# Another order of the first loads and other planner numbers in a fused attention and gMLP kernel

## Chip, core and metric

The kernel runs on one core of a Trainium2 chip. The metric is the device time of one execution in microseconds; lower is better. A program of this kind has one launch, and all inputs start in the chip's main memory.

## The reference

Chunked attention (batch 4, 8 heads, 768 positions, head size 64) feeds a gMLP block. Each chunk of 32 queries sees 16 positions to its left, itself, 8 to its right, and 8 memory keys of its head.

```python
for c in range(nc):                       # 24 chunks
    k_full = concat([mem_k, k[l_start:r_end]]); v_full = concat([mem_v, v[l_start:r_end]])
    a = softmax(scale * q_c @ k_full.T)
    out[c] = a @ v_full
x = out, heads side by side               # [4, 768, 512]
h = relu(x @ w_in)                        # w_in [512, 1024]
u, v = h[..., :512], h[..., 512:]
v_n = (v - mean(v)) / sqrt(var(v) + 1e-6)
v_s = einsum('ts,bsd->btd', w_spatial, v_n) + b_spatial
return (u * v_s) @ w_out                  # w_out [512, 512]
```

w_in and w_out come in 64-bit floats; the kernel makes them 32-bit.

## The kernel before

**Tiles.** The tokens go through attention in 24 tiles of four chunks (128 positions, all heads): per tile a burst of 64 small matmuls for the scores of tile i and 64 for the values of tile i-1 (`burst`, line 419), a softmax on VectorE and ScalarE (lines 472 to 493), two transposes (lines 507 and 523), and the result x split into a rounded high and a low half (lines 528 and 532), since each product is made of three matmuls: high by high, low by high, high by low. Queries and keys come in groups of two tiles (`load_qk`), and group 0 in two units of one tile. Values come per tile (`load_v`, four or more DMAs).

**gMLP.** `ffn_v` multiplies a tile of x by the v half of w_in (four chunks of 128 rows by three matmuls, lines 561 to 563, 512 columns each), and its result is normalized and stored to main memory (`vn_far`). `ffn_u` multiplies three tiles of x by a quarter of the u half (384 columns), with chunks 0 to 3 in this order too. Later phases read both back (`near_v`, `near_u`) for the spatial product and the output product, each in seven partial products instead of eight (line 710).

**w_in.** `w_in_part(c, part, ...)` loads one part, rows c of four and the half `part` (0 is u, 1 is v), 512 KB as 64-bit words, into one of four `big` buffers, and makes 32-bit values: a scale on ScalarE (line 864), two shift operations on VectorE (lines 873, 874), a second scale on ScalarE (869), an addition on GpSimd (879), which frees the `big` buffer; then a rounded high half on ScalarE (893) and a low half (897), on VectorE for v-parts and on GpSimd for u-parts. The arguments after c and part are the rank of this work, the rank of the load and the engine of the low half.

**The order.** Nothing runs in the order of the source. `Plan.op` collects every operation with an engine, an expected time, what it reads and writes, and a rank. `Plan.order` then simulates the engines: each time it takes the operation that can start first, and among equals the lowest rank. What comes out is the order in which each engine's instructions are issued; on the chip each engine keeps to it and waits on semaphores. So an expected time that is off doesn't change what is computed, only what stands ahead of what. A load's expected end is the end of a pipe that moves `mb * drag / rate` us for each transfer, plus `landing`. Loads with `seq=True` keep the order of the source on SP's queue; each loop or call that makes them stands at the end of the file (lines 968 to 1003). `alone` keeps a VectorE operation from starting in the plan while GpSimd is busy, and GpSimd from starting until it ends; the two first shift operations are one planned operation of this kind.

**Pacing.** `held_by` limits what is in flight: a transfer waits until so many of the earlier ones have landed that it and the rest are within a window of megabytes. The window goes by what has been issued so far. The same function makes real waits in `transfer` and expected ones in the plan. q and k count 1.15 times their size, v 1.2 times.

**Filler.** Where the plan leaves TensorE idle between 9 and 36 us, `busy` (line 252) issues matmuls on the identity.

Of the kernel before, what the change touches and what calls it, by code (L numbers as in the profile page):

```python
# [10 lines left out]
U32 = mybir.dt.uint32  # L11
# [8 lines left out]
SLOT = 40  # L20
LEFT = 16
WIN = 64
MIDDLE = (38.0, 1.2)
PIECES = 4
NEG = -1.0e30

# [1 line left out]
class Plan:  # L28
# [111 lines left out]
    def held_by(self, flight, mb, none):  # L140

        moved = sum(size for _, size in flight)
        window = self.early[1] if moved <= self.early[0] else MIDDLE[1] if moved < MIDDLE[0] else self.window
        for back, (name, size) in enumerate(reversed(flight), 1):
            mb += size
            if back == 8 and moved > self.early[0] or mb > window:
                return name
        return none
# [10 lines left out]
def tile_chunked_attention_gmlp(  # L159
# [43 lines left out]

    sizes = {"f": 3, "sx": 1, "pt": 1, "xt": 1, "y": 5, "st": 9, "big": 4, "uo": 2, "x": 2, "vm": 3,
             "q": 2, "k": 2, "kT": 2, "p": 1, "xs": 1, "pT": 1, "vr": 2, "op": 4, "sm": 2, "ug": 6, "ot": 11}
    plan = Plan(sizes, {"f", "y", "st", "big", "ot"}, rate=0.30, landing=2.5, lat=0.06, window=1.75, early=(9.0, 2.0))
    op = plan.op

    def act(n):
# [56 lines left out]
    def src(t, offset, ap):  # L266
        return bass.AP(tensor=t.tensor, offset=offset, ap=ap)
# [20 lines left out]
    def load(dst, src_, w, rank, r=(), eng="SP", slow=1.0, us=0.45, seq=False, drag=1.0, of=None):  # L288
        e = {"SP": nc.sync, "ACT": nc.scalar, "POOL": nc.gpsimd}[eng]
        n = 4  # L290
        for s in src_.shape:
            n *= s
        mb = n / 1e6 * slow
        n = op(eng, us, lambda: transfer(e, dst() if callable(dst) else dst, src_, mb, of), r=r, w=w, rank=rank, mb=mb,
               after=line.get(eng) if seq else None, drag=drag)
        if seq:
            line[eng] = n
# [15 lines left out]
    def load_qk(g, units=(0, 1), seq=True):  # L313
        i = 2 * g
        b, c0 = i // UB, (i % UB) * UC
        off = b * H * D * S + c0 * CH
        nk = 2 * UT + CH
        lo = LEFT if c0 == 0 else 0
        hi = nk - LEFT if c0 + 2 * UC == NC else nk
        q0, q1 = units[0] * UT, units[-1] * UT + UT  # L320
        k0, k1 = max(lo, q0 + (CH if q0 else 0)), min(hi, q1 + CH)
        u = units[0]
        ks = ("k", g)
        n = PIECES if g > 1 else 1
        for t in range(n):
            ts = slice(t * T // n, (t + 1) * T // n)
            load(lambda ts=ts: spot("q", g, [P, T, 2 * UT])[:, ts, q0:q1],
                 src(q, off + q0 + ts.start * P * S, [[S, P], [P * S, T // n], [1, q1 - q0]]), w=[("q", g, u, t)], rank=10.0 * i,
                 slow=1.15, seq=seq)
        for t in range(n):  # L330
            ts = slice(t * T // n, (t + 1) * T // n)
            load(lambda ts=ts: spot("k", g, [P, T, nk])[:, ts, k0:k1],
                 src(k, off - LEFT + k0 + ts.start * P * S, [[S, P], [P * S, T // n], [1, k1 - k0]]), w=[("k", g, u, t)],
                 rank=10.0 * i, slow=1.15, seq=seq)

        def pad():
            a = t_["k", g]
            if k0 == lo > 0:
                nc.gpsimd.memset(a[:, :, 0:lo], 0.0)
            if k1 == hi < nk:  # L340
                nc.gpsimd.memset(a[:, :, hi:nk], 0.0)
        if k0 == lo > 0 or k1 == hi < nk:
            op("POOL", 0.2, pad, w=[ks + (u, "pad")], rank=10.0 * i, after=len(plan.ops) - 1)
# [203 lines left out]
    seq = [0]  # L547
# [305 lines left out]
    def from_f64(name, src_, rank, load_rank, home, after=()):  # L853
        big = ("big", *name)
        zk = ("st", ("z", name))

        def get():
            a = alloc("big", big, [P, 2 * DH], U32).rearrange("p (c w) -> p c w", w=2)
            t_[big] = a
            return a  # L860
        load(get, src_.bitcast(U32).rearrange("p (c w) -> p c w", w=2), w=[("big", big)], r=after, rank=load_rank, seq=True)

        def scale_():
            nc.scalar.activation(alloc("st", ("z", name), [P, DH], F32), t_[big][:, :, 1].bitcast(F32), AF.Copy,
                                 scale=2.0 ** -112)

        def rest():
            a = t_[big][:, :, 0]
            nc.scalar.activation(a, a, AF.Copy, scale=2.0 ** -29)

        def shift():
            zu = t_["st", ("z", name)].bitcast(U32)
            nc.vector.tensor_scalar(zu, zu, 3, None, op0=ALU.logical_shift_left)  # L873
            nc.vector.scalar_tensor_tensor(zu, t_[big][:, :, 1], 0x80000000, zu,  # L874
                                           op0=ALU.bitwise_and, op1=ALU.bitwise_or)

        def add():
            zu = t_["st", ("z", name)].bitcast(U32)
            nc.gpsimd.tensor_tensor(t_[big][:, :, 1] if home else zu, zu, t_[big][:, :, 0], op=ALU.add)
        op("ACT", 0.66, scale_, r=[("big", big)], w=[zk], rank=rank)  # L880
        op("DVE", 1.12, shift, r=[("big", big)], w=[zk], rank=rank, alone=True)
        op("ACT", 0.66, rest, r=[("big", big)], w=[("big", big, "r")], rank=rank)
        op("POOL", 1.6 if home else 1.35, add, r=[("big", big, "r"), zk] if home else [("big", big, "r")],
           w=[("big", big)] if home else [zk], rank=rank)
        if home:
            return (lambda: t_[big][:, :, 1].bitcast(F32)), ("big", big)
        return (lambda: t_["st", ("z", name)]), zk
# [14 lines left out]
    def w_in_part(c, part, rank, load_rank, sub_eng):  # L902
        cols = slice(part * DH, (part + 1) * DH)
        z, zk = from_f64(("win", c, part), w_in[c * P:(c + 1) * P, cols], rank, load_rank, False)
        split(sub_eng, DH, lambda x: (win_l if x else win_h)[:, c, cols], z, [zk], [("win", c, part)], rank)
# [64 lines left out]
    for j in range(NV):  # L970
        spread_mem(j, "DVE" if j < 1 else "POOL", 1.0 + 10 * j)
    load_qk(0, (0,))
    load_qk(0, (1,))
    w_in_part(0, 1, 5.0 + 0, 2.0 + 0, "DVE")
    w_in_part(1, 1, 5.0 + 1, 2.0 + 1, "DVE")
    w_in_part(2, 1, 5.0 + 2, 2.0 + 2, "DVE")
    w_in_part(3, 1, 5.0 + 3, 2.0 + 3, "DVE")
    load_v(0)
    load_qk(1)
    w_in_part(0, 0, 25.0 + 0, 15.0 + 0, "POOL")  # L980
    load_v(1)
    w_in_part(1, 0, 25.0 + 1, 15.0 + 1, "POOL")
    load_v(2)
    w_in_part(2, 0, 25.0 + 2, 15.0 + 2, "POOL")
    w_in_part(3, 0, 25.0 + 3, 15.0 + 3, "POOL")
    for j in range(NK):
        spread_keys(j, 1.0 + j)
    for i in range(NU + 1):
# [23 lines left out]
    for b in range(B + 1):  # L1012
        if b < B:
            rank = 300.0 + 10 * b
# [67 lines left out]
```

## Time and profile before

| what | us |
|---|---|
| median of 3 runs | 379.18 |
| lowest and highest of these | 376.54, 381.41 |
| the profiled execution | 375.05 |
| its span, first to last instruction | 373.3 |
| mean granted clock of TensorE in it | 0.999 of full speed |

The span is the part of the profiled execution that its rows describe. PE is the matrix engine (TensorE), PEld its loading of weights, DVE is VectorE, ACT ScalarE, POOL GpSimd, SP the engine that issues most DMAs; a q behind an engine's name is its queue. In a row `win_l<-st,win_h` names the written tile first.

### The profile page before, as it was taken

The page shows a single profiled execution, that of the slowest core. Times are in us where ns is not written, and L with a number is a line of the kernel's source. Part 1 is how long each engine was busy: PE and PEld are TensorE (multiplying, and loading weights), DVE is VectorE, ACT ScalarE, POOL GpSimd, SP SyncE. Part 2 cuts the span into 40 slices and gives each one's busy share as a digit, 9 for nine tenths or more (in the row PEclk, how much of TensorE's full clock was granted, in tenths as well). Part 3 has the DMA queues.
Part 4 walks back from the last instruction along what each step waited for, and adds up shares of the span by engine and source line. Part 5 has one row for each costly group of instructions (what it writes and reads, how often), then busy time and mean ns, then how long its engine had stood idle before and what let it go on. Part 6 is the DMA issues. An engine that isn't in the chain of part 4 may idle for free.

```text
span 373.3 us, 11922 instructions
## 1 busy us (share of the span) xinstructions
PE 355.9 (95%) x4988; PEld 326.7 (88%) x4988; DVE 285.0 (76%) x479; ACT 187.1 (50%) x334; POOL 160.5 (43%) x155
## 2 busy tenths in 40 slices
PE   2987989999999999999999999999999999999995
PEld 2865877998988978979889898999999999999995
DVE  3888856748758568566598589999969896898893
ACT  3768435454555454554473355346434743744371
POOL 6446642374386077520042194961256025106500
PEclk9999999999999999999999999999999999999999
DMA  8995888778787765886742648205720662230014
GB/s 230 316 260 140 232 257 210 235 217 220 228 251 214 249 212 147 274 232 194 216 163 93 246 137 311 88 2 173 246 90 3 207 217 84 84 130 2 0 54 159
DMA packets 48517, 65.52 MB, mean 176 GB/s; under 512 B 5456, under 2 KB 39888, under 8 KB 48464
## 3 DMA queue, kind: packets, MB, share of 16 engines
q1 hardware_dynamic: 47808, 64.44, 56.5%
q8 instruction: 39, 0.64, 0.8%
q10 hardware_dynamic: 656, 0.33, 0.3%
q14 instruction: 14, 0.11, 0.1%
HBM read 45.88 MB, written 18.87 MB: 173 GB/s over the span
## 4 chain that ended last, share of the span: by engine, by line
PE 83%; DVE 11%; ACT 2%; issue 2%; DMA 1%; SPq 0%; ACTq 0%; DVEq 0%
PE y L710 21%; PE f L710 15%; PE f L561 12%; PE f L562 11%; PE f L563 11%; PE sx L419 9%; PE xt L523 3%; PE pt L507 3%; DVE op L690 2%; DVE sm L673 2%; DMA k<-in_k_dram 1%; DVE st L874 1%; DVE st L873 1%; DVE wout L897 1%; DVE p L480 1%
## 5 line engine op out<-in xcount | busy, mean ns | idle before, releaser
L710 PE MATMUL y<-wsp,op 128*128 128x384 f32 x288 | 52.0, 336 | 0.9 <-ACT st L750 0.9
L764 POOL TENSOR_TENSOR ug<-st,ug 128x384 f32<-128x384 f32 x24 | 36.0, 1513 | 38.4 <-DVE st L756 34.4
L710 PEld LDWEIGHTS y<-wsp,op 128*128 128x128 f32 x288 | 49.9, 188 | 1.2 <-ACT st L750 1.2
L561 PE MATMUL f<-x,win_h 128*128 128x384 f32 x128 | 46.1, 360 | 0.0
L563 PE MATMUL f<-x,win_h 128*128 128x384 f32 x128 | 43.2, 337 | 0.0
L562 PE MATMUL f<-x,win_l 128*128 128x384 f32 x128 | 43.1, 337 | 0.0
L561 PE MATMUL f<-win_h,x 128*128 128x512 f32 x96 | 40.8, 425 | 0.0
L710 PE MATMUL f<-wsp,op 128*128 128x384 f32 x216 | 39.4, 336 | 0.0
L562 PE MATMUL f<-win_h,x 128*128 128x512 f32 x96 | 37.9, 394 | 1.0 <-DVE x L532 1.0
L563 PE MATMUL f<-win_l,x 128*128 128x512 f32 x96 | 37.7, 392 | 0.0
L710 PEld LDWEIGHTS f<-wsp,op 128*128 128x128 f32 x216 | 37.6, 188 | 0.0
L690 DVE TENSOR_TENSOR op<-sm,op 128x768 fp32r<-128x768 f32 x32 | 34.7, 1093 | 3.1 <-ACT op L687 2.6
L710 PE MATMUL y<-wout,op 128*128 128x256 f32 x288 | 35.9, 281 | 0.5 <-DVE op L690 0.5
L459 DVE TENSOR_TENSOR xs<-sx,rec 128x512 f32<-128x512 f32 x24 | 16.5, 687 | 25.1 <-PE sx L419 25.0
L710 PEld LDWEIGHTS y<-wout,op 128*128 128x128 f32 x288 | 34.7, 188 | 1.0 <-DVE op L690 0.8
L770 POOL TENSOR_TENSOR st<-st,bias 128x384 f32<-128x384 f32 x14 | 18.6, 1337 | 37.2 <-ACT st L750 28.4
L597 POOL TENSOR_TENSOR rstd<-ve,mhalf 128x1 f32<-128x1 f32 x24 | 14.7, 611 | 44.7 <-DVE ve L593 43.6
L687 ACT CAST op<-sm 128x768 fp32r<-128x768 f32 x32 | 26.2, 837 | 11.6 <-DVE sm L673 10.2
L419 PEld LDWEIGHTS sx<-kmain,q 64*32 64x32 f32 x1536 | 17.0, 107 | 14.8 <-issue 11.7
L622 ACT ACTIVATE uo<-f 128x384 f32<-128x384 f32 x32 | 15.6, 492 | 25.2 <-PE f L563 21.9
L398 POOL COPY vmain<-memv 8x1024 f32<-8x1024 f32 x22 | 23.9, 1090 | 10.0 <-PE sx L419 7.8
L419 PE MATMUL sx<-kmain,q 64*32 64x64 f32 x1536 | 20.9, 228 | 7.3 <-ACT kmain L404 7.0
(86 smaller groups left out, 770.6 us busy)
## 6 DMA issues: line engine op xcount, KB each, us to landing
vmain<-in_v_dram SPq DMA_DIRECT2D x48, 128.0 KB
vn_far<-st SPq DMA_DIRECT2D x24, 256.0 KB
u_far<-uo SPq DMA_DIRECT2D x32, 192.0 KB
vr<-vn_far SPq DMA_DIRECT2D x8, 768.0 KB
ug<-u_far SPq DMA_DIRECT2D x16, 384.0 KB
q<-in_q_dram SPq DMA_DIRECT2D x40, 128.0 KB
vmain<-in_v_dram SPq DMA_DIRECT2D x47, 96.0 KB
out_dram<-ot SPq DMA_DIRECT2D x33, 128.0 KB
```

The source lines that it names most:

```text
L398: ins = {"DVE": nc.vector, "POOL": nc.gpsimd}[eng].tensor_copy(to, of)
L419: ins = nc.tensor.matmul(o, w_, m, start=True, stop=True, skip_group_check=True)
L459: nc.vector.tensor_tensor(xs.rearrange("p t r d -> p r t d"), t_["sx", i][:, :, 1], rec.rearrange("p t r -> p r t").unsqueeze(3).broadcast ...
L561: nc.tensor.matmul(o, lh, rh, start=(j == 0), stop=False)
L562: nc.tensor.matmul(o, ll, rh, start=False, stop=False)
L563: nc.tensor.matmul(o, lh, rl, start=False, stop=(j == len(pairs) - 1))
L622: op("ACT", act(HT), lambda: nc.scalar.activation(alloc("uo", i, [P, HT], F32), t_["f", n], AF.Relu), r=[("f", n)], w=[("uo", i)], rank=rank)
L687: nc.scalar.copy(half(0), of())
L690: nc.vector.tensor_tensor(half(1), of(), half(0).bitcast(F32), op=ALU.subtract)
L710: nc.tensor.matmul(o, x, y, start=first and m == 1, stop=m == 3 * chunks, skip_group_check=True)
L764: nc.gpsimd.tensor_tensor(g, t_[st(x)], g, op=ALU.mult)
L770: {"DVE": nc.vector, "POOL": nc.gpsimd}[eng].tensor_tensor(a, a, bias[:, 1], op=ALU.add)
```

## The change

The first loads get another order: u-part 2 of w_in comes second among w_in's parts, both v-part 0 and u-part 2 ahead of unit 1 of the first queries and keys; v-part 1 comes behind the first values; u-part 0 becomes the last. The ranks of u-parts go from 25 + c to 28 + c. In the planner a landing takes 2.0 us instead of 2.5, the 64-bit loads of w_in and w_out are expected to take 0.7 of the time by size, and the narrow window of 1.2 MB begins at 10.5 MB moved instead of 9.0 (between them the window is 1.75 MB).

```diff
--- before.py
+++ after.py
@@ -20,7 +20,7 @@
 SLOT = 40
 LEFT = 16
 WIN = 64
-MIDDLE = (38.0, 1.2)
+MIDDLE = (10.5, 38.0, 1.2)
 PIECES = 4
 NEG = -1.0e30
 
@@ -140,7 +140,7 @@
     def held_by(self, flight, mb, none):
 
         moved = sum(size for _, size in flight)
-        window = self.early[1] if moved <= self.early[0] else MIDDLE[1] if moved < MIDDLE[0] else self.window
+        window = self.early[1] if moved <= self.early[0] else MIDDLE[2] if MIDDLE[0] < moved < MIDDLE[1] else self.window
         for back, (name, size) in enumerate(reversed(flight), 1):
             mb += size
             if back == 8 and moved > self.early[0] or mb > window:
@@ -203,7 +203,7 @@
 
     sizes = {"f": 3, "sx": 1, "pt": 1, "xt": 1, "y": 5, "st": 9, "big": 4, "uo": 2, "x": 2, "vm": 3,
              "q": 2, "k": 2, "kT": 2, "p": 1, "xs": 1, "pT": 1, "vr": 2, "op": 4, "sm": 2, "ug": 6, "ot": 11}
-    plan = Plan(sizes, {"f", "y", "st", "big", "ot"}, rate=0.30, landing=2.5, lat=0.06, window=1.75, early=(9.0, 2.0))
+    plan = Plan(sizes, {"f", "y", "st", "big", "ot"}, rate=0.30, landing=2.0, lat=0.06, window=1.75, early=(9.0, 2.0))
     op = plan.op
 
     def act(n):
@@ -858,7 +858,7 @@
             a = alloc("big", big, [P, 2 * DH], U32).rearrange("p (c w) -> p c w", w=2)
             t_[big] = a
             return a
-        load(get, src_.bitcast(U32).rearrange("p (c w) -> p c w", w=2), w=[("big", big)], r=after, rank=load_rank, seq=True)
+        load(get, src_.bitcast(U32).rearrange("p (c w) -> p c w", w=2), w=[("big", big)], r=after, rank=load_rank, seq=True, drag=0.7)
 
         def scale_():
             nc.scalar.activation(alloc("st", ("z", name), [P, DH], F32), t_[big][:, :, 1].bitcast(F32), AF.Copy,
@@ -970,19 +970,19 @@
     for j in range(NV):
         spread_mem(j, "DVE" if j < 1 else "POOL", 1.0 + 10 * j)
     load_qk(0, (0,))
+    w_in_part(0, 1, 5.0 + 0, 2.0 + 0, "DVE")
+    w_in_part(2, 0, 28.0 + 2, 15.0 + 2, "POOL")
     load_qk(0, (1,))
-    w_in_part(0, 1, 5.0 + 0, 2.0 + 0, "DVE")
-    w_in_part(1, 1, 5.0 + 1, 2.0 + 1, "DVE")
     w_in_part(2, 1, 5.0 + 2, 2.0 + 2, "DVE")
     w_in_part(3, 1, 5.0 + 3, 2.0 + 3, "DVE")
     load_v(0)
+    w_in_part(1, 1, 5.0 + 1, 2.0 + 1, "DVE")
     load_qk(1)
-    w_in_part(0, 0, 25.0 + 0, 15.0 + 0, "POOL")
     load_v(1)
-    w_in_part(1, 0, 25.0 + 1, 15.0 + 1, "POOL")
+    w_in_part(1, 0, 28.0 + 1, 15.0 + 1, "POOL")
     load_v(2)
-    w_in_part(2, 0, 25.0 + 2, 15.0 + 2, "POOL")
-    w_in_part(3, 0, 25.0 + 3, 15.0 + 3, "POOL")
+    w_in_part(3, 0, 28.0 + 3, 15.0 + 3, "POOL")
+    w_in_part(0, 0, 28.0 + 0, 15.0 + 0, "POOL")
     for j in range(NK):
         spread_keys(j, 1.0 + j)
     for i in range(NU + 1):
```

## Rows read from the trace of the kernel before

**Rows 1.** Page part 1: busy us, share of the span, instructions.
```profile
PE 355.9 (95%) x4988; PEld 326.7 (88%) x4988; DVE 285.0 (76%) x479; ACT 187.1 (50%) x334; POOL 160.5 (43%) x155
```

**Rows 2.** By stretch: us, busy PE, PEld, DVE, ACT, POOL; PEclk, DMA share, GB/s.
```profile
7.00:24.00 17.00, 15.86 (x309) 12.65 (x310) 15.22 (x26) 11.04 (x20) 8.76 (x7) 1.00 1.04 312
24.00:41.00 17.00, 14.72 (x333) 11.06 (x315) 14.96 (x31) 11.49 (x20) 9.70 (x9) 1.00 0.70 190
41.00:60.00 19.00, 17.79 (x397) 15.37 (x396) 11.26 (x21) 8.75 (x16) 8.47 (x12) 1.00 0.86 234
60.00:230.00 170.00, 168.60 (x3016) 149.52 (x3015) 121.78 (x242) 87.02 (x154) 76.89 (x82) 1.00 0.69 213
230.00:373.00 143.00, 138.86 (x962) 138.07 (x960) 120.58 (x158) 66.54 (x123) 53.33 (x38) 1.00 0.32 106
```

**Rows 3.** The chain that ended last, its end: start us, us, what.
```profile
365.13 4.21 PE f L710 x36
```

**Rows 4.** Line 252 alone, the filler matmuls: us, PE, PEld, then as rows 2.
```profile
7.00:24.00 17.00, 11.29 (x42) 8.45 (x42) 1.00 1.04 312
24.00:41.00 17.00, 0.60 (x2) 0.30 (x2) 1.00 0.70 190
```

**Rows 5.** Waits of TensorE: waited for, us in total, times, longest us.
```profile
PE sx L419 <- ACT kmain L404: 7.0, 1, 7.0
...
PE f L562 <- DVE x L532: 1.0, 1, 1.0
```

**Rows 6.** Timeline from 8 to 28 us: start us, us, engine, line, operation.
```profile
8.15 0.72 ACT L404 COPY kmain<-k 128x640 f32<-128x640 f32 x1 [1.28 <-DMA k<-in_k_dram]
...
16.83 0.62 ACT L485 ACTIVATE p<-p 128x512 f32<-128x512 f32 x1
...
18.48 1.67 DVE L874 SCALAR_TENSOR_TENSOR st<-big,st 128x512 uint32<-128x512 uint32 x1
...
23.21 0.62 ACT L893 CAST win_h<-st 128x512 fp32r<-128x512 f32 x1
...
23.86 0.69 DVE L897 TENSOR_TENSOR win_l<-st,win_h 128x512 fp32r<-128x512 f32 x1 [0.32 <-ACT win_h L893]
...
24.16 0.50 PE L561 MATMUL f<-win_h,x 128*128 128x512 f32 x1
...
24.36 0.66 ACT L864 ACTIVATE st<-big 128x512 f32<-128x512 f32 x1
...
26.81 0.39 PE L563 MATMUL f<-win_l,x 128*128 128x512 f32 x1
```

**Rows 7.** Timeline of SP's DMA issues: start us, us for all of a row.
```profile
35.11 0.35 SPq L281 DMA_DIRECT2D vn_far<-st  x1
...
37.42 1.85 SPq L281 DMA_DIRECT2D k<-in_k_dram  x4
```

**Rows 8.** VectorE's groups, 24 to 41 us: busy us, mean ns.
```profile
L874 DVE SCALAR_TENSOR_TENSOR st<-big,st 128x512 uint32<-128x512 uint32 x4 | 2.8, 693 | 0.1
...
L873 DVE TENSOR_SCALAR st<-st 128x512 uint32<-128x512 uint32 x4 | 1.7, 418 | 0.0
```

**Rows 9.** Timeline of GpSimd: addition, then first and last low half of u.
```profile
18.25 1.35 POOL L879 TENSOR_TENSOR st<-st,big 128x512 uint32<-128x512 uint32 x1 [1.15 <-DVE st L874]
...
28.62 1.28 POOL L897 TENSOR_TENSOR win_l<-st,win_h 128x512 fp32r<-128x512 f32 x1 [0.95 <-ACT win_h L893]
...
44.34 1.30 POOL L897 TENSOR_TENSOR win_l<-st,win_h 128x512 fp32r<-128x512 f32 x1 [0.20 <-ACT win_h L893]
```

**Rows 10.** Timeline from 34 to 42 us, around x tile 2.
```profile
34.79 0.59 ACT L528 CAST x<-xt 128x512 fp32r<-128x512 f32 x1 [0.23 <-PE xt L523]
...
35.45 0.69 DVE L874 SCALAR_TENSOR_TENSOR st<-big,st 128x512 uint32<-128x512 uint32 x1
...
36.66 0.68 DVE L532 TENSOR_TENSOR x<-xt,x 128x512 fp32r<-128x512 f32 x1
...
41.48 0.34 PE L561 MATMUL f<-x,win_h 128*128 128x384 f32 x1
```

## The prediction

> **What bounds the kernel now.** I read the busy table first: TensorE 355.9 of 373.3 us [rows 1]. The table by stretches says where the other time is [rows 2]: from 60 to 230 us it misses 1.40 us, and from 230 on 4.14 us, of which 3.66 lie behind the last matmuls, which end at 369.34 [rows 3]. So the body is bound by TensorE, and a change of order there can win 1.40 + 0.48 = 1.9 us at most. The head is different. Of the 15.86 us "busy" in 7 to 24, 11.29 are filler matmuls on the identity, so only 4.57 are work; in 24 to 41 it is 14.72 - 0.60 = 14.12 of 17 [rows 2, 4]. What is lost in the head is 7.0 + 12.4 + 2.9 = 22.3 us. It is bound by data and by VectorE: the DMA engines are full in 7 to 24 (share 1.04, 312 GB/s), and VectorE has 15.22 and 14.96 of 17 us [rows 2]. The waits of TensorE name the first keys (7.0 us, the whole of 0 to 7) and, later, the low half of x (1.0 us) [rows 5]. The first gMLP group starts at 24.16, just as the low half of the fourth v-part of w_in is made (23.86 to 24.55) [rows 6]. Behind that wait for x, from 37.4 on, TensorE is all but full.
>
> **Step 1, the landings.** One w_in part is 0.524 MB, and so is unit 1 of the first q and k (2 x 0.262); at 312 GB/s that is 1.68 us; a set of v (0.459 MB) is 1.47, q and k of group 1 (1.114 MB) 3.57. Unit 1's keys were there at 8.15 [rows 6]. From that anchor, by sums of sizes: before, the v-parts 0 to 3 land at 9.8, 11.5, 13.2, 14.9, v(0) at 16.3, group 1 at 19.9, and the u-parts at 21.6, 24.7, 27.9, 29.5. After: v-part 0 at 8.1, u-part 2 at 9.8, unit 1 at 11.5, v-parts 2 and 3 at 13.2 and 14.9, v(0) still 16.3, v-part 1 at 18.0, group 1 at 21.6, u-parts 1, 3, 0 at 24.7, 27.9, 29.5. The bytes are the same, eight w_in issues stay eight, and SP's 0.35 to 0.46 us an issue [rows 7] is far below the 1.68 us that a part takes to move.
>
> Unit 1 is 3.4 us later. It is needed for the second burst of scores, whose softmax was not urgent: its exponential ran only at 16.83 [rows 6]. I cost this at nothing; if the cover were gone it would be the 3.4.
>
> The last v-part is v-part 1, 3.1 us later. Behind its landing it needs, bare, scale 0.66, two shift operations 0.42 + 0.69, the addition on GpSimd 1.35, the rounding 0.62 and the low half 0.69, 4.4 us together [rows 6, 8, 9], so 22.4, where the same point is 24.55 now: slack 2.1 us. As chunk 1 of four comes last, chunks 1 to 3 (nine matmuls) follow it. Twelve took from 24.16 to 27.20 [rows 6], 0.25 each, so nine take 2.3 us: done at 24.7 to 26.9 against 27.20. Cost 0; if the slack is gone, up to 3.1.
>
> **Step 2, u-part 2 early.** Into 7 to 24 come 0.42 + 0.69 = 1.11 us of VectorE and, if its low half is made there too, 1.35 + 1.30 us of GpSimd [rows 8, 9]. VectorE has 17 - 15.22 = 1.78 us idle there, and v-part 0 comes 1.7 us sooner, so it can begin sooner. That hides it: I take 0. Best case, the chain moves by the whole 1.7 us. Worst case, the cover is gone and VectorE also waits for both GpSimd operations: +1.11 + 2.65 = +3.8. I take the value of the idle row, 0, and keep -1.7 and +3.8.
>
> A stretched row shows the second price. The shift operation of 0.69 took 1.67 us at 18.48, while GpSimd had an addition in work from 18.25 (1.35) [rows 6, 8, 9]: it ended at 20.15, 0.55 behind GpSimd's 19.60. [...]
>
> **Step 3, one part less in 24 to 41.** The shift of the third u-part (its second operation from 35.45) stood with another operation ahead of the low half of x tile 2: that had its input at 34.79 + 0.59 = 35.38 and ran at 36.66, 1.28 us late [rows 10], and a matmul waited 1.0 us for it [rows 5]. With one of four conversions done before 24, VectorE is 1.11 us lighter up to this point, so TensorE fills 1.1 to 1.3 us sooner: I take -1.2. Ends: 0 (another operation stands there), and -2.9 (all that the stretch loses).
>
> **Step 4, the u-halves.** Of four low halves the first ended at 29.90 and the last at 45.64, so they were (45.64 - 29.90) / 3 = 5.2 us apart [rows 9]. Three are left; the first lands at 24.7, and the first now took 5.5 us from its scale (24.36 [rows 6]) to 29.90, so 30.2, then 35.4 and 40.7; packed tight (1.11 + 1.35 + 0.62 + 1.30 = 4.4 apart) 39.0. A u-group takes the chunks in the order 0 to 3, and chunk 0 now lands last, so no u-group can start before that. Now they start at 41.48 [rows 10]; 1.2 sooner is 40.3. The middle of 39.0 and 40.7 is 39.9: cost 0. The ranks 28 + c put part 3 behind attention tile 3, which has 30, so VectorE serves that first; it is part of the 5.2. The cover here is thin; rival A is its price.
>
> **Step 5, the pacing between 9.0 and 10.5 MB.** By the sizes with their factors, 8.50 MB are moved with the first loads and 9.05 with v(3). The next, q and k of group 2, 1.28 MB, pass from a window of 1.2 MB to 1.75: a first piece (0.15) with v(3) (0.55) and one w_in part (0.52) is 1.23. So it need no longer wait for a w_in part that the planner expects late, and should pass the first vn_far store, which waits on SP until 35.11 with q and k behind it to 37.42 [rows 7]. The DMA engines gain a filled hole; TensorE gains nothing, since it has 17.79 of 19 us in 41 to 60 [rows 2] and these keys feed burst 4 there: 0. The store comes some 3.7 us later behind eight issues of 0.46; nobody reads it for long.
>
> **Step 6, landing 2.0 and 0.7 for f64 parts.** They only change the order in the queues, from the head to the end (w_out's loads too). The gain is bounded by the 1.9 us above. For a loss there is no row of its own; TensorE's idle time between 41 us and its last matmul is 1.21 + 1.40 + 0.48 = 3.1 us now [rows 2, 3], and I bound it by as much again. Value 0.
>
> **Sum.** 0 + 0 - 1.2 + 0 + 0 + 0 = -1.2 us. The profiled execution has 375.05 us, so 373.85; the median of the runs is 4.13 above it, so 377.98, which I give as 378.0.
>
> **Rivals.** A, the u-halves come last: chunk 0's low half ends where the last ends now, 45.64, and TensorE stands from 40.3. From 44.5 it has the v-group of tile 3 (twelve matmuls, 3.0 us), whose x is about then made, and fills the last 1.1 of the 5.3: +4.2 on the forecast, 382.2, slower than now by 3.0. It decides from the moment that chunk 0 is later than 40.3. For it: chunk 0 lands last and four chunks were 5.2 apart. Against: one less to convert.
> [...]
> C, the plan fits the chip better all along: -1.7 (step 2), -2.9 (step 3), -1.9 (step 6) = -6.5, 372.7. For it: the DMA rate in the head is nearly what the new numbers say. Against: all three must come whole.
> D, the change doesn't do what it says: the early part lands but its conversion (rank 30) waits, so VectorE has the same order of work: 0, 379.2.
>
> **Chances.** Forecast 0.42, A 0.17, B 0.15, C 0.16, D 0.10. The runs before spread from 376.54 to 381.41, so each case has about 1 us to either side. The range 371.8 to 383.8 takes in the unknown bounds of A and C but for their tails. About what a measurement of this kernel can tell is 2%, 7.6 us: faster than 371.6 needs C and more, 0.05; slower than 386.8 needs A with B or a loss in step 6, 0.06; within 0.89.
>
> **What would show it.** Right: u-part 2's scale on ScalarE before 13 us, its addition on GpSimd before 18; the first v-group still at 23.5 to 24.7; the x tile 2 stall gone and TensorE full from about 36.2; the last u low half at 38.9 to 40.7 and no idle before the first u-group; q and k of group 2 issued ahead of the first store, near 29 us; the same 1.4 us of idle in 60 to 230. [...]

## The result and the profile after

The changed kernel took a median of 380.25 us (22 runs, 375.64 to 382.30) beside 376.57 us for the kernel before (22 runs, 374.79 to 381.41): a ratio of 1.0083, 95% interval 1.0058 to 1.0108. (Medians are of all runs; this ratio and those below leave out the runs that are more than 1.5% above the fastest of their kernel.) The forecast was 1.2 us less; it is some 3 to 4 us more. That is small, but it has the other sign, so the question is which terms failed. The forecast's 378.0 also stood on a median of three runs, 379.18, which lies 2.6 us above that of the 22; from 376.57 the same -1.2 gives 375.4. The profiled execution of after took 380.31 us, its median; that of before, 375.05, lies 1.5 under its own. So the two spans, 378.5 and 373.3, differ by 5.2 us where the medians differ by 3.7.

By stretches, the kernel after (us, busy PE, PEld, DVE, ACT, POOL; granted clock, DMA share, GB/s):

```profile
7.00:24.00 17.00, 14.71 (x236) 11.10 (x222) 15.11 (x25) 11.28 (x20) 9.01 (x8) 0.90 1.03 280
24.00:41.00 17.00, 14.77 (x369) 10.85 (x369) 16.13 (x28) 11.68 (x22) 7.88 (x9) 1.00 0.93 225
41.00:60.00 19.00, 17.10 (x393) 14.66 (x392) 13.05 (x27) 8.37 (x16) 10.36 (x13) 1.00 0.93 236
60.00:230.00 170.00, 165.24 (x2992) 145.51 (x2991) 116.38 (x232) 83.74 (x149) 71.89 (x78) 1.00 0.66 200
230.00:378.00 148.00, 144.39 (x992) 143.44 (x990) 127.81 (x166) 70.16 (x128) 54.79 (x41) 1.00 0.35 115
```

Beside [rows 2] the 5.2 us fall into three parts. From 60 us on TensorE still has 165.24 + 144.39 = 309.63 us to do, where it had 168.60 + 138.86 = 307.46: the first 60 us do 2.2 us less. Between 60 and 230 it now idles 4.76 us instead of 1.40: 3.4 us. From 230 to the end of the span it idles 4.1 instead of 4.4: -0.3. The sum is 5.2. The end itself is the same piece as in [rows 3], 4.21 us, starting at 370.67.

The 2.2 us can be counted. Line 561 alone, up to 60 us, first before, then after (us; PE and PEld busy with counts; clock, DMA share, GB/s):

```profile
0.00:60.00 60.00, 12.45 (x32) 6.00 (x32) 1.00 0.86 237
```
```profile
0.00:60.00 60.00, 11.56 (x29) 5.45 (x29) 0.97 0.93 240
```

Each chunk of a gMLP group starts with one matmul of this line and has three in all: 29 chunks are begun instead of 32. They are not all whole: of the 512-column matmuls of lines 561 to 563, 250 are left from 60 us on instead of 244 (of the 384-column ones as many as before), six at some 0.4 us, 2.4 us. I use this count below for "work of the head", and the idle time of TensorE from 60 to 230 us for "the body".

The head of after, from its timeline (start us, us, engine, line, operation):

```profile
9.33 0.68 ACT L864 ACTIVATE st<-big 128x512 f32<-128x512 f32 x1
...
10.99 0.71 ACT L404 COPY kmain<-k 128x640 f32<-128x640 f32 x1
...
13.71 1.29 POOL L879 TENSOR_TENSOR st<-st,big 128x512 uint32<-128x512 uint32 x1 [1.42 <-ACT st L864]
...
17.39 0.97 PE L419 MATMUL sx<-vmain,pT 64*32 64x64 f32 x64 [1.95 <-DMA vmain<-in_v_dram]
...
19.63 0.67 ACT L864 ACTIVATE st<-big 128x512 f32<-128x512 f32 x1 [2.01 <-DMA big<-in_moe_w_in_dram]
...
23.85 0.73 ACT L404 COPY kmain<-k 128x640 f32<-128x640 f32 x1 [0.42 <-DMA k<-in_k_dram]
...
25.41 0.51 PE L561 MATMUL f<-win_h,x 128*128 128x512 f32 x1
...
26.94 0.68 DVE L897 TENSOR_TENSOR win_l<-st,win_h 128x512 fp32r<-128x512 f32 x1
```

The early part is converted as meant (scale 9.33, addition 13.71). But the values of tile 0 arrive only for 17.39, and TensorE stands 1.95 us for them, a wait that before did not have (the burst itself is not late: before it ran at 18.36, behind filler); v-part 1's scale waits 2.01 us for its load and runs at 19.63, and its low half, the last of the v-parts, ends at 27.62 instead of 24.55 [rows 6]. The first gMLP group starts 1.25 us later.

The body of after: waits of TensorE from 60 to 230 us (waited for, us in total, times, longest), and the timeline at the longest of them:

```profile
PE sx L419 <- issue: 2.3, 2, 2.0
PE pt L507 <- ACT p L485: 1.1, 1, 1.1
PE xt L523 <- DVE xs L459: 0.8, 1, 0.8
PE xt L523 <- DVE p L480: 0.6, 1, 0.6
```
```profile
111.78 0.57 PE L419 MATMUL sx<-vmain,pT 64*32 64x64 f32 x34
...
114.34 0.30 PE L419 MATMUL sx<-vmain,pT 64*32 64x64 f32 x4 [1.99 <-issue]
```

Before, the same stretch had 0.9 us for an output operand (line 750) and 0.5 of "issue". The new waits are of two kinds: softmax work that comes late (2.5 us), and 1.99 us in the middle of a burst of small matmuls, where nothing that the trace shows holds TensorE.

### The profile page after: what moved, and what is told of

It is laid out like the page before. It is cut to its first block, busy times and chain, and to the rows that moved or that the text cites. A ratio compares the mean times of both kernels' runs of the same rounds, so it can differ in the third digit from the quotient of the medians.

```text
span 378.5 us, 11910 instructions
## 1 busy us (share of the span) xinstructions
PE 356.4 (94%) x4976; PEld 325.8 (86%) x4976; DVE 289.9 (77%) x479; ACT 187.4 (50%) x334; POOL 157.4 (42%) x155
## 4 chain that ended last, share of the span: by engine, by line
PE 73%; DMA 14%; DVE 5%; ACT 3%; SPq 3%; issue 2%; ACTq 0%; DVEq 0%
PE y L710 22%; PE f L710 15%; PE f L561 9%; PE f L562 8%; PE f L563 8%; PE sx L419 6%; DMA vmain<-in_v_dram 4%; DMA k<-in_k_dram 4%; SPq L281 3%; DMA big<-in_moe_w_spatial_dram 2%; PE xt L523 2%; PE pt L507 2%; DMA big<-in_moe_w_in_dram 2%; DMA big<-in_moe_w_out_dram 1%; DVE op L690 1%
## 5 line engine op out<-in xcount | busy, mean ns | idle before, releaser
L764 POOL TENSOR_TENSOR ug<-st,ug 128x384 f32<-128x384 f32 x24 | 33.9, 1432 | 35.1 <-DVE st L756 31.3
L585 ACT ACTIVATE st<-f 128x512 f32<-128x512 f32 x24 | 14.3, 598 | 32.6 <-PE f L563 32.1
```

Source lines behind the costliest of these rows:

```text
L764: nc.gpsimd.tensor_tensor(g, t_[st(x)], g, op=ALU.mult)
```

## The experiments

Three questions: which part costs the head its 2.2 us, which costs the body its 3.4 us, and whether either has to do with this change at all. The table holds all 18 further kernels, nearly in the order in which they are told; the ratio is to the kernel before, from the same chips.

| kernel | median us | ratio (95%) | chunks by 60 us | idle 60-230, us |
|---|---|---|---|---|
| before | 376.57 | 1 | 32 | 1.40 |
| after | 380.25 | 1.0083 (1.0058-1.0108) | 29 | 4.76 |
| e1_order | 387.11 | 1.0313 (1.0273-1.0353) | 24 | 6.49 |
| e2_numbers | 381.98 | 1.0190 (1.0145-1.0235) | 28 | 1.12 |
| e4_nodrag | 385.92 | 1.0268 (1.0227-1.0310) | 23 | 4.77 |
| e5_middle9 | 378.59 | 1.0023 (0.9975-1.0071) | 32 | 2.23 |
| e3_landing25 | 379.40 | 1.0068 (1.0032-1.0105) | 30 | 4.56 |
| e6_chunks | 380.86 | 1.0100 (1.0060-1.0140) | 29 | 2.00 |
| e7_v1_early | 389.77 | 1.0321 (1.0276-1.0366) | 28 | 6.75 |
| e8_null | 379.42 | 1.0061 (1.0027-1.0094) | 31 | 3.56 |
| e9_null_order | 383.73 | 1.0135 (1.0079-1.0191) | 32 | 3.42 |
| e10_after_lat065 | 384.93 | 1.0227 (1.0168-1.0285) | 28 | 4.21 |
| e11_before_lat055 | 385.56 | 1.0211 (1.0128-1.0293) | 33 | 3.26 |
| e12_after_lat055 | 382.14 | 1.0148 (1.0101-1.0195) | 30 | 2.11 |
| e13_unit1_first | 381.23 | 1.0083 (1.0035-1.0131) | 32 | 5.17 |
| e14_u2_late | 381.01 | 1.0109 (1.0046-1.0171) | 26 | 2.57 |
| e15_u2_late_v1_early | 380.80 | 1.0114 (1.0065-1.0163) | 28 | 4.19 |
| e16_code64 | 386.65 | 1.0268 (1.0201-1.0335) | | |
| e17_code32 | 381.69 | 1.0106 (1.0056-1.0156) | | |
| e18_before_code64 | 386.65 | 1.0277 (1.0201-1.0352) | | |

(The last two columns come from each kernel's one profile. Those of before, e2, e5, e6, e11 and e12 are of executions 1.2 to 4.1 us faster than the kernel's median, that of e4 of one 5.1 us slower. The last three have extra work in front and are read at their waits.)

### Order, numbers, and each number

**e1_order** has the new order of loads and ranks with the planner numbers of before; **e2_numbers** has the old order with the new numbers.

```diff
# e1_order, against after
-MIDDLE = (10.5, 38.0, 1.2)
+MIDDLE = (38.0, 1.2)
-    plan = Plan(..., rate=0.30, landing=2.0, lat=0.06, ...)
+    plan = Plan(..., rate=0.30, landing=2.5, lat=0.06, ...)
-        load(get, ..., rank=load_rank, seq=True, drag=0.7)
+        load(get, ..., rank=load_rank, seq=True)
# e2_numbers, against before: the same lines the other way round
```

> The new order of loads and the new ranks alone, the planner's numbers as before. Theory N (the loss behind 60 us comes from the planner's numbers): only the head's loss is there, so +1.8 us (ratio 1.005), idle TensorE from 60 to 230 us at most 2 us, the first v-group near 25.4. Theory O (the order carries it all): ratio 1.008 to 1.010 and over 4 us idle in 60 to 230.

> The planner's numbers alone (landing 2.0, 0.7 for 64-bit loads, narrow window from 10.5 MB), the loads in the old order. Theory N: the head as before (first v-group near 24.2, 32 first-of-three matmuls of the gMLP by 60 us) and over 4 us idle in 60 to 230: ratio 1.006 to 1.009. Theory O: ratio 1.000, idle there about 1.4.

Measured: +3.1% and +1.9%, while both together cost +0.8%. Neither theory had such figures, and e2, with its loads in the old order, has only 28 chunks: the numbers alone can cost the head as much. So the parts don't add: new numbers help the new order (387.1 to 380.3) and hurt the old one (376.6 to 382.0). e2's profile happens to be of its fastest execution (377.84 against a median of 381.98), so its row in the table flatters it.

**e4_nodrag**, **e5_middle9** and **e3_landing25** each take one number back from after.

```diff
# e4_nodrag
-        load(get, ..., rank=load_rank, seq=True, drag=0.7)
+        load(get, ..., rank=load_rank, seq=True)
# e5_middle9
-MIDDLE = (10.5, 38.0, 1.2)
+MIDDLE = (9.0, 38.0, 1.2)
# e3_landing25
-    plan = Plan(..., rate=0.30, landing=2.0, lat=0.06, ...)
+    plan = Plan(..., rate=0.30, landing=2.5, lat=0.06, ...)
```

> The changed kernel without the 0.7 for 64-bit loads. If the 0.7 makes the plan too early in the head, the 1.95 us wait for the values near 15.4 goes and the first v-group comes before 25; ratio about 1.004. If landing or the order is the cause: 1.008, and the wait stays.

> The changed kernel with the narrow window from 9.0 MB again, as before. If the wider window costs or gives anything by itself, q and k of group 2 go back behind the first store and the ratio leaves 1.008 by more than 0.007; by theory G it is one more new order of the same family: 1.000 to 1.015, with 2 to 6 us of idle TensorE from 60 to 230 us.

> The changed kernel with landing 2.5 again. If the optimistic landing is what puts TensorE's instructions ahead of their data, idle in 60 to 230 falls from 4.8 to about 1.4 us and the ratio to about 1.004; if it is the 0.7 or the window, nothing moves: 1.008.

Measured: 1.0268, 1.0023, 1.0068. Without the 0.7 the new order is 1.8% slower than with it, which neither of e4's two expectations had. Its profile shows 23 chunks, though of an execution of 391.05 us, above its median, so that count is less sure. The 0.7 is the number that the new order lives on; that it works by letting the planner expect the f64 parts sooner is argued, not shown. The landing time does nothing that can be told from after. With the old pacing the median is 378.59; its interval meets that of after, so no gain is shown. Its queue is of use for step 5, below.

### Chunk order and the place of v-part 1

**e6_chunks** lets both kinds of group take the chunks in the order in which they are loaded. **e7_v1_early** puts v-part 1 back ahead of the values.

```diff
# e6_chunks (in ffn_v; in ffn_u the same with (2, 1, 3, 0))
-        n = group(DH, [lambda c=c: pair(c) for c in range(KT)],
+        n = group(DH, [lambda c=c: pair(c) for c in (0, 2, 3, 1)],
# e7_v1_early
     w_in_part(3, 1, 5.0 + 3, 2.0 + 3, "DVE")
+    w_in_part(1, 1, 5.0 + 1, 2.0 + 1, "DVE")
     load_v(0)
-    w_in_part(1, 1, 5.0 + 1, 2.0 + 1, "DVE")
```

> The changed kernel with the gMLP groups taking the chunks in the order in which they now land: v 0, 2, 3, 1 and u 2, 1, 3, 0. If the late chunks 1 and 0 at the wrong places of the groups cost the head its 1.8 us, the gMLP has 31 to 33 first-of-three matmuls by 60 us instead of 29 and the ratio falls to about 1.003. If the head is late because the last part itself is late, 29 to 30 and 1.008.

> The changed kernel with v-part 1 again ahead of v-part 2 and of the first values. If the late v-part 1 is what moved the first v-group from 24.2 to 25.4, it is back at 24.2 to 24.6, and the ratio falls to about 1.004; if it is the early u-part or the later unit 1, it stays at 25.4 or later and the values come 1.7 us later too: 1.008 or more.

e6: 1.0100, 29 chunks, as after. Which chunk comes last (rival A's price, and the slack of step 1) is not what costs the head. e7: 1.0321, the slowest of all, with 28 chunks: v-part 1's late place is not the cause either; moved forward it delays the values, whose burst waits 1.73 us for its load and runs at 21.38, and the first group starts at 27.91.

### Is it the change at all? Four pairs

**e8_null** and **e9_null_order** are the kernel before with one planner constant moved a little, a change that asks nothing else of the chip than another order (in e9 it is `lat`, the time that the planner adds where one engine takes over from another); **e11_before_lat055** is a third. **e10_after_lat065** and **e12_after_lat055** move the same constant in after.

```diff
# e8_null, against before
-    plan = Plan(..., rate=0.30, landing=2.5, lat=0.06, ...)
+    plan = Plan(..., rate=0.30, landing=2.4, lat=0.06, ...)
# e9_null_order, against before: lat=0.065
# e11_before_lat055, against before: lat=0.055
# e10_after_lat065, against after: lat=0.065
# e12_after_lat055, against after: lat=0.055
```

> The kernel before with landing 2.4 instead of 2.5, a change that means nothing for the chip but makes the planner write another order. Theory G (any new order meets the chip worse than the one before, whose numbers were fitted to it): idle TensorE from 60 to 230 us grows from 1.4 to 3 to 6 us, ratio 1.005 to 1.02. Theory S (the loss is special to the change's numbers): ratio 0.997 to 1.003 and idle there under 2 us.

> The kernel before with the planner's latency 0.065 instead of 0.06 us, a second change of that kind. Theory G: ratio 1.005 to 1.02, idle from 60 to 230 us 3 to 6 us. Theory S: 0.997 to 1.003 and under 2 us.

> The changed kernel with the planner's latency 0.065 instead of 0.06. Theory G: the changed kernel is an ordinary member of its family, so this lies to either side of 1.008, between 1.000 and 1.018, with 28 to 31 first-of-three matmuls by 60 us. Theory S: it stays at 1.006 to 1.010 with the same idle of 4.8 us from 60 to 230 us.

> The kernel before with the planner's latency 0.055. Theory G: slower than before as its two sisters were, 1.003 to 1.015, over 3 us idle from 60 to 230 us, with 32 or more first-of-three matmuls by 60 us, since the loads are in the old order. Theory S: 0.997 to 1.003.

> The changed kernel with the planner's latency 0.055. Theory G: 1.000 to 1.018 and 28 to 31 first-of-three matmuls by 60 us. Theory S: 1.006 to 1.010 with 4.8 us idle from 60 to 230 us.

These settle most. Every small redraw of the old kernel is slower than it: by 0.6, 1.35 and 2.1% (e11, and e10 beside after, lie beyond what theory G allowed). Their heads are unchanged (31 to 33 chunks, first group at 23.92 to 24.06), and their bodies idle 3.26 to 3.56 us, where the kernel before idles 1.40. By stretch, the body of e8_null:

```profile
60.00:230.00 170.00, 166.44 (x3000) 146.60 (x2999) 119.19 (x236) 85.44 (x151) 74.75 (x79) 1.00 0.69 204
```

For e9 and e11 the body is less than half of their loss. Their longest waits stand behind it, where the spatial product waits for its operand `op`; in e11:

```profile
233.37 0.69 PE L710 MATMUL y<-wsp,op 128*128 128x384 f32 x1 [5.47 <-ACT op L687]
```

All four kernels with another `lat` (e9 to e12) stand 3.0 to 5.8 us there, between 228 and 245 us, and their mean granted clock from 230 to 372 us is 0.98 or 0.99, where before and after have 1.00. TensorE idles 7.2 to 8.0 us from 230 us on in them, 4.4 in before and 4.1 in after. So the column "idle 60-230" understates what such a redraw costs.

Set side by side, old order and numbers against new, at equal settings: lat 0.06, 1 and 1.0083; lat 0.055, 1.0211 and 1.0148; lat 0.065, 1.0135 and 1.0227; landing near 2.5 (e8 and e3), 1.0061 and 1.0068. The differences are +0.0083, -0.0063, +0.0092 and +0.0007, in the mean +0.3% with a standard error of 0.4%. So over redraws the change is worth nothing that four pairs can show. The head, however, is worse in all four: 32, 33, 32, 31 chunks against 29, 30, 28, 30, in the mean 2.75 fewer. In 512-column matmuls left from 60 us on (244, 241, 242, 245 against 250, 250, 252, 248) that is 7 more, some 2.8 us, 0.7%: a price of the change as a whole. That it is the order's alone is not shown, as e2 (old order, 28 chunks) and e5 (new order, 32) stand against it. The body (means 2.91 and 3.91 us) is mostly a draw, in which the kernel before did best of eight; what is drawn is told under "The waits with no releaser".

### Which move costs the head

**e13_unit1_first** puts only unit 1 of q and k back in front. **e14_u2_late** puts only u-part 2 back behind the keys of group 1, as the first of the u-parts. **e15_u2_late_v1_early** does that and moves v-part 1 ahead of v-part 2.

```diff
# e13_unit1_first
     load_qk(0, (0,))
+    load_qk(0, (1,))
     w_in_part(0, 1, 5.0 + 0, 2.0 + 0, "DVE")
     w_in_part(2, 0, 28.0 + 2, 15.0 + 2, "POOL")
-    load_qk(0, (1,))
# e14_u2_late
-    w_in_part(2, 0, 28.0 + 2, 15.0 + 2, "POOL")
...
     load_qk(1)
+    w_in_part(2, 0, 28.0 + 2, 15.0 + 2, "POOL")
     load_v(1)
# e15: as e14, and
     load_qk(0, (1,))
+    w_in_part(1, 1, 5.0 + 1, 2.0 + 1, "DVE")
...
     load_v(0)
-    w_in_part(1, 1, 5.0 + 1, 2.0 + 1, "DVE")
```

> The changed kernel with unit 1 of the first queries and keys again ahead of v-part 0 and u-part 2. The measure is the start of the last low half of the v-parts on VectorE (before 23.9, changed 26.9). Theory M (the late unit 1 between the 64-bit parts slows the DMA engines and holds attention): 25 or earlier. Theory U (the early u-part costs it): 26.5 or later, as v-part 0 is 2 us later too. Ratio 1.000 to 1.02 by the draw of the order behind it.

> The changed kernel with u-part 2 behind group 1, as the first of the u-parts again, and all else as changed (v-part 1 still behind the first values). Theory U: the last low half of the v-parts starts at 23.5 to 24.9, at least 2 us sooner than 26.9, and the gMLP has 31 or more first-of-three matmuls by 60 us. Theory V (the late v-part 1 costs it): 26 or later.

> As the one before, and v-part 1 ahead of v-part 2 again: of the new order only v-part 0 ahead of unit 1 and u-part 0 as the last are left. Theory U: within 0.7 us of the one before. Theory V: 23 to 24, 2 us or more sooner than the one before.

By the measure that was set, the start of the last low half of the v-parts (26.94 in after), e13 has 28.50, on theory U's side; e14 has 25.54, between U and V, with 26 chunks where U had 31; e15 has 28.24, outside both. So none of the theories came out by that measure, and what follows was read afterwards. The DMA rates say what happens. By 2 us, from 8 us on: before, after, e13 (columns as in the first table of this section):

```profile
8.00:10.00 2.00, 2.00 (x15) 1.57 (x6) 1.55 (x3) 0.84 (x2) 1.83 (x2) 1.00 1.05 404
10.00:12.00 2.00, 2.00 (x70) 1.26 (x69) 1.35 (x4) 1.67 (x3) 0.00 (x0) 1.00 0.98 384
```
```profile
8.00:10.00 2.00, 2.00 (x5) 1.64 (x6) 1.89 (x4) 1.91 (x4) 1.75 (x2) 1.00 1.08 323
10.00:12.00 2.00, 1.66 (x31) 0.73 (x38) 1.57 (x4) 1.87 (x5) 1.00 (x1) 1.00 1.00 292
```
```profile
8.00:10.00 2.00, 1.49 (x27) 0.60 (x11) 1.59 (x4) 1.21 (x2) 1.99 (x2) 1.00 1.02 406
10.00:12.00 2.00, 1.69 (x67) 1.55 (x68) 1.77 (x5) 1.86 (x4) 0.39 (x1) 1.00 1.03 391
```

The engines are equally full (share 0.98 to 1.08), but w_in parts in a row moved at 384 to 406 GB/s, and with unit 1 of q and k among them it was 292 to 323. Part of this is only moved in time, as before has unit 1 at 6 to 8 us (329 GB/s, after 370): from 6 to 12 us it is 372 GB/s before, 328 after, 373 in e13. The other kernels agree: with unit 1 in front (before, e2, e8, e9, e11, e13) the rate from 8 to 12 us is 394 to 414 and five of six have 31 to 33 chunks, with unit 1 behind (after and ten others) it is 280 to 345 and ten of eleven have 23 to 30. In e13 the rate is back, and so are the 32 chunks: its values burst runs at 17.49 without the wait, its last v-part is scaled at 18.05, and the low half of x tile 0 is made at 20.47 where after has 24.63:

```profile
17.49 0.86 PE L419 MATMUL sx<-vmain,pT 64*32 64x64 f32 x64
...
18.05 0.67 ACT L864 ACTIVATE st<-big 128x512 f32<-128x512 f32 x1 [1.54 <-DMA big<-in_moe_w_in_dram]
...
20.47 0.69 DVE L532 TENSOR_TENSOR x<-xt,x 128x512 fp32r<-128x512 f32 x1
...
21.43 0.48 PE L561 MATMUL f<-win_h,x 128*128 128x512 f32 x1
...
28.50 0.69 DVE L897 TENSOR_TENSOR win_l<-st,win_h 128x512 fp32r<-128x512 f32 x1
```

Against this stands its last v low half, at 28.50, later than in after: by that point alone unit 1 would not be the cause. I go by the count of chunks, which is what TensorE got done, but I chose it after the run. e14 and e15, with u-part 2 late, have 26 and 28 chunks, so taking the early u-part out gave none back. Each is one draw of the planner; e5 reached 32 chunks with the new order too, and e2 only 28 with the old. So unit 1 is the likeliest cause, not a proven one. e13's time stayed at 1.0083 as its body drew 5.17.

### The waits with no releaser

Where does "issue" in the middle of a burst come from? The page of after lists the transfers of instructions:

```profile
q8 instruction: 39, 0.64, 0.8%
```

That is 39 packets of 16 KB (0.64 MB in all), and TensorE has 4976 + 4976 = 9,952 matmuls and weight loads, 255 for each packet. Counted along all of TensorE's recorded rows (these and some hundred waits of its queue), the waits inside bursts came at rows 1985 and 4289 in after and 961, 1730 and 5313 in before. To within one row they lie 9, 3 and 14 times 256 apart, so 256 is the piece I count by: all five stand at position 193 or 194 of one. At the wait of 112.35 to 114.34 one such packet is in the queues (112.00 to 112.88); the list for 112 to 113 us:

```profile
q8 instruction: 1, 0.02, 5.5%
```

Theory: each packet is one such piece of TensorE's code, a burst runs through 128 instructions in 0.86 us, and where it meets the end of a piece, TensorE stands until the next one is there. Rival: these waits belong to the place in the order, through something that the trace doesn't show. To tell them apart, small matmuls on the identity were put in front: each ran as two matmuls and two weight loads (5,104 matmul rows in e16, 4,976 in after), so 64 shift all that follows by 256 instructions, one whole piece, and 32 by half a piece. The expectations had counted half of that: e16 and e18 were meant to move the waits, and by a whole piece could not. The test is e17.

```diff
# e16_code64 against after, e18_before_code64 against before; e17_code32: range(32)
+        for _ in range(64):
+            nc.tensor.matmul(idle[0:CH, 0, 0:D], ident[0:D, 0:CH], ident[0:D, 0:D], start=True, stop=True, ...)
```

> The changed kernel with 64 small matmuls on the identity put ahead of everything, where TensorE waits for the first keys anyway: the same order on every engine, but TensorE's code lies 128 instructions further on. Theory C (waits of TensorE that name no releaser, such as the 1.99 us at 112.35, are waits for its own code, which comes in pieces): they change place and size, the 1.99 us goes to under 0.5 us or another burst, while the waits for VectorE and ScalarE at 147.5, 170.6 and 190.9 (2.5 us) stay within 0.4 us each. Theory D (these waits belong to the order or the data): all waits stay within 0.4 us.

> As the one before with 32 small matmuls, 64 instructions. Theory C: the waits without a releaser are again others, so the idle time from 60 to 230 us is 2.5 us plus another amount, 0 to 4 us. Theory D: 4.8 us as in the changed kernel.

> The kernel before with the 64 small matmuls. Theory C: its waits without a releaser (0.96 at 31.0, 0.90 at 52.5, 0.52 at 136.4, 2.4 us together) are others, between 0 and 6 us together, and the ratio lies between 0.995 and 1.012. Theory D: the same waits at the same places, ratio 0.998 to 1.002.

The times are spoilt: 64 matmuls took 13.75 us and 32 took 6.92, and the first scores came 8 and 1.2 us later. The positions are not. First e18, then before, at the same burst:

```profile
38.96 0.33 PE L419 MATMUL sx<-vmain,pT 64*32 64x64 f32 x13
...
42.76 1.06 PE L419 MATMUL sx<-vmain,pT 64*32 64x64 f32 x51 [3.48 <-issue]
```
```profile
30.69 0.33 PE L419 MATMUL sx<-vmain,pT 64*32 64x64 f32 x13
...
31.99 0.75 PE L419 MATMUL sx<-vmain,pT 64*32 64x64 f32 x51 [0.96 <-issue]
```

A whole piece leaves the cut after the 13th of 64 matmuls in both; likewise e16 stops four matmuls before the end of the burst in which after stops there (2.25 us at 119.00). Half a piece moves it: e17 has no such wait in the burst in which after and e16 stop, and one of 1.63 us in another burst, from 74.17, at position 194 again:

```profile
73.44 0.72 PE L419 MATMUL sx<-vmain,pT 64*32 64x64 f32 x51
...
75.80 0.33 PE L419 MATMUL sx<-vmain,pT 64*32 64x64 f32 x11 [1.63 <-issue]
...
114.79 0.82 PE L419 MATMUL sx<-vmain,pT 64*32 64x64 f32 x62
```

The rival, by which the place in the order decides, would have left e17's where it was. Two counts agree. With one more piece of instructions the page of e16 lists one more packet, as does that of e18:

```profile
q8 instruction: 40, 0.66, 0.8%
```

And of the 71 waits of TensorE over 0.2 us that name no releaser, in all 20 traces, 63 stand at position 193 or 194. They are not confined to bursts: 3.03 us in e7 stand at a matmul of a gMLP group, right behind two bursts:

```profile
87.12 0.68 PE L561 MATMUL f<-x,win_h 128*128 128x384 f32 x1 [3.03 <-issue]
```

Few ends of pieces cost time: of the 783 in the 20 traces 720 cost under 0.2 us, and the other 63 cost 0.2 to 3.5 us each (5 of 78 in before and after). Of after's extra 3.4 us of body, 1.99 - 0.52 = 1.5 are of this kind (its second wait, 0.27 us, stands elsewhere). In the other kernels of the four pairs such waits take, of the idle time from 60 to 230 us, 3.0 us in e8, 3.3 in e9, 3.6 in e3, 3.1 in e10, 0.4 in e12 and none in e11. So of the 2.3 us that the seven bodies idle more than that of before in the mean, 1.7 are such waits at the ends of pieces, and not an order that fits the chip worse. One and the same end can differ: before's 0.96, 0.90 and 0.52 us are 3.48, 1.48 and under 0.2 in e18. That TensorE waits there for its code fits e17 and the packets, but no trace shows what it waits for. Why one end costs time and another does not stays open, and with one profile for each kernel no run shows how much they differ from one execution to the next.

## Why the prediction was wrong, by its steps

**Step 1 failed, and it is the likeliest cause of the head's loss.** It spread all landings at 312 GB/s, the mean of [rows 2]; after moved 280 in that stretch. The rate went with what was moved beside what: 404 and 384 GB/s before, 323 and 292 after, at shares of 0.98 to 1.08. So "the bytes are the same" did not make the times the same. The first landings still came about as forecast (v-parts 2 and 3 were scaled at 12.94 and 15.08, for 13.2 and 14.9); the later ones, at 262 GB/s from 12 to 24 us, did not. v-part 1 was forecast to land at 18.0, with its scale then; it ran at 19.63. Group 1 was to land at 21.6; its first keys were copied at 23.85. The first late u-part was to land at 24.7, and its scale waited for the load until 28.73. The slack of 2.1 us was also counted with 4.4 us "bare" on a VectorE that [rows 2] show full (15.22 of 17 us): from the scale to the end of the low half it took 27.62 - 19.63 = 8.0 us. And "unit 1 is 3.4 us later ... I cost this at nothing" named the wrong cover. That unit 1's keys came 2.8 us later (10.99 against 8.15) may indeed have hurt nobody; its rows among the w_in parts are what e13 points to. The head, for which this step had 0, costs some 2.8 us over the four pairs, order and numbers together.

**Step 2 held in its mechanism.** u-part 2 was converted before 24 us, apart from its low half at 24.11, and e14 and e15 show no gain in chunks from taking it out (in e14 the last v low half comes 1.4 us sooner). Its best case, the chain 1.7 us sooner, is not seen.

**Step 3 failed.** The 1.2 us, all of the forecast gain, rested on VectorE being 1.11 us lighter behind 24. It is not: 16.13 us busy in 24 to 41, where before has 14.96 [rows 2], although two conversions less stand there. v-part 1's work slid in (two v low halves start behind 24 us, where before has none), and four operations that run beside GpSimd are stretched by 2.8 us together (two by 0.9 before), such as these two of 0.69 and 0.17 us:

```profile
24.11 1.76 POOL L897 TENSOR_TENSOR win_l<-st,win_h 128x512 fp32r<-128x512 f32 x1
...
25.23 1.18 DVE L897 TENSOR_TENSOR win_l<-st,win_h 128x512 fp32r<-128x512 f32 x1
...
40.06 1.30 POOL L897 TENSOR_TENSOR win_l<-st,win_h 128x512 fp32r<-128x512 f32 x1
40.09 1.30 DVE L491 TENSOR_TENSOR den<-den,eps 128x8 f32<-128x8 f32 x1
```

The low half of x tile 2 is made at 37.76, 1.1 later than in [rows 10], and TensorE waits 0.99 us near there for a softmax:

```profile
37.71 0.66 PE L507 MATMUL pt<-ident,p 128*128 128x128 f32 x4 [0.99 <-ACT p L485]
37.76 0.68 DVE L532 TENSOR_TENSOR x<-xt,x 128x512 fp32r<-128x512 f32 x1
...
44.49 0.34 PE L561 MATMUL f<-x,win_h 128*128 128x384 f32 x1
...
47.14 1.30 POOL L897 TENSOR_TENSOR win_l<-st,win_h 128x512 fp32r<-128x512 f32 x1
```

**Step 4 was off in its times, right in its cost.** The last u low half ends at 48.44, not at 38.9 to 40.7, and u-groups start at 44.49, not 40.3. The last one is not chunk 0's, which a u-group needs first: chunk 0 landed last but was not converted last, and its low half is the third, done at 41.36. That is 1.1 us behind the 40.3 from which rival A was to decide, and A's price did not come: v-groups filled the time, TensorE's one wait near 40 is 0.91 us, and e6, which takes chunk 0 last, gains nothing.

**Step 5 was right in its outcome and wrong in its reason.** q and k of group 2 do pass the first store:

```profile
32.12 3.08 SPq L281 DMA_DIRECT2D q<-in_q_dram  x4
35.48 2.45 SPq L281 DMA_DIRECT2D k<-in_k_dram  x4
38.03 0.38 SPq L281 DMA_DIRECT2D vn_far<-st  x1
```

They go at 32, not 29, and in e5, with the old pacing, they also go first (34.27 against the store's 37.75). So the window between 9.0 and 10.5 MB is not what lets them pass. In the three redraws of before (e8, e9, e11) the store is first, as in [rows 7].

**Step 6 failed in its value.** It was bounded by "as much again", 3.1 us, and the body's loss is 3.4; I took 0 because landing and factor "only change the order". Any change of the order is a new draw: of the eight kernels of the four pairs, the one before idles 1.40 us in the body and the other seven 2.11 to 4.76, in the mean 3.70. The order of before has the least idle time of them, so zero was the wrong value for a term that re-writes it; 3.70 - 1.40 = +2.3 us is what a redraw costs there, 1.7 of it in waits at the ends of pieces, which no term had, and behind 230 us four of the seven lose some 3 us more. Landing alone (e3) moved nothing; the 0.7 (e4) is worth 1.8% to the new order, by its one profile through the head and not the body.

**The rivals.** B, by which GpSimd's work for the early part was to lengthen VectorE's before 24 us, did not come: one shift took 1.66 us at 18.32, as one did before (1.67 in [rows 6]), and VectorE has 15.11 us in 7 to 24, beside 15.22 in [rows 2]. Stretched operations show behind 24 us (step 3: 2.8 us in four); what that costs in time no run separates. By how much differs: beside the two GpSimd operations in step 3, of 1.76 and 1.30 us, VectorE's took 0.49 and 1.13 us longer. C came in no kernel. D is excluded by the scale at 9.33. With steps 1 and 6 at the middle of their own bounds (0 to 3.1, and -1.9 to 3.1) the same sum would have been 1.55 + 0.6 - 1.2 = +0.95 us, and had the right sign; that would still have been luck, as it has neither the waits at the ends of pieces nor the rate.

## What to carry to other kernels

In a kernel whose order comes from a planner, a neutral change of a planner constant should be timed beside the change that one wants to judge: here neutral redraws cost 0.6 to 2.1%, mostly more than the change, and all three redraws of the kernel before were slower than it. Compare a change with redraws of its base, not with the base alone. A full share of the DMA engines is not a rate (here 404 GB/s at a share of 1.05, 292 at 1.00): price a reordering of loads with the GB/s of a stretch in which the same neighbours were moved, not with the mean. Read a term "it only changes the order" as a loss of the size of the idle time that the other draws have, not as zero. And before an order is blamed for a wait in the middle of a burst, count the instructions ahead of it: here 63 of the 71 waits over 0.2 us with no releaser stood at position 193 or 194 of 256.

## What the runs showed of the hardware

Three things were unexpected. TensorE stood 0.2 to 3.5 us with no releaser in the trace at 63 of 783 positions that lie 256 recorded rows apart; the five such waits of before and after are all inside bursts of 64 by 64 matmuls, and in e17, with half a piece more in front, the longest, 1.63 us, stood in another burst than the longest of after, 1.99 us. The same 16 DMA engines moved 404 GB/s (before, 8 to 10 us, share 1.05) or 292 (after, 10 to 12 us, share 1.00), with other loads side by side in the queue. And after TensorE's 1.95 us without work ahead of 17.39 its granted clock fell to 0.50 of full speed:

```profile
18.00:20.00 2.00, 2.00 (x31) 1.70 (x15) 1.95 (x2) 0.37 (x1) 1.35 (x1) 0.50 0.95 285
20.00:22.00 2.00, 2.00 (x7) 1.41 (x5) 1.63 (x3) 1.85 (x4) 0.38 (x1) 0.66 1.10 285
```

It was back at 1.00 from 22 us on. Filler was 2.80 of the 4.00 us that TensorE is busy in these two rows, so I take it to have cost little here; before, with no such wait, [rows 2] have 1.00 in the same stretch. Not every wait of that size does it: after stands 1.99 us ahead of 114.34, and the granted clock stays at 1.00 behind it (114 to 122 us).
